# A third gate bank, mirrors one step late, and output products brought forward at the change to pairs

## The chip, the cores and the metric

The kernel runs on one core of a Trainium2 chip. The metric is the device time of one execution in microseconds (us). Medians of several executions are given, and all executions here are in the fast state (granted TensorE clock 0.997 to 1.000 of full speed). A profile is one execution. Its times are counted from the start of its span, and the span is about 2 us shorter than the time that is reported for the same execution.

## The reference, cut to what matters

```
X   = fft(fft(x, axis=1), axis=2).real      # x: 8 x 3008 x 256
gate = relu(X @ w_gate);  val = X @ w_val   # 256 -> 1536
out  = (gate * val) @ w_out                 # 1536 -> 256
```

The kernel works on 24 blocks (8 sequences, 3 blocks each) of up to 512 columns, and on 12 slices of 128 hidden units per block. A spectrum of real data is symmetric, so each block serves direct rows and mirrored rows. A gate is the sum of an even and an odd part; adding one further matmul with the odd weights times minus two (`wm`) into the same PSUM bank turns the direct gate into the mirrored one.

## The kernel before: the parts concerned

The names used below: t counts slices over all blocks, and the first block is t = 0 to 11. G(t) are the two gate matmuls, M(t) the gate's mirror matmul, W(t) the value's mirror matmul, V(t,0) and V(t,1) the two value matmuls. gs(t) and gm(t) are ScalarE's relus of the direct and the mirrored gate. direct_h and mirror_h are VectorE's products, and E(t) is VectorE's even part of the value, from t = 12 on. Output products are the matmuls of h with the output weights `wo`. Stage 1 and stage 2, transposes and weight folding prepare transforms and weights, and their matmuls stand between the others. The prelude is all that comes before the first gate matmul. A bank is the part of PSUM, the memory into which TensorE writes its sums, that holds one tile of 128 x 512 numbers.

```
psg = tile_pool(bufs=2)          # gate banks
pso = tile_pool(bufs=1)          # output banks, two tags
ps1 = singles.tile_pool(bufs=4)  # value banks of the first block, also of the prelude
# ... cut

def gate(t):
    G = Gt[t] = psg.tile([128, 512], F32, tag="g")
    matmul(G, wc[0], ..., start=True);  matmul(G, ws[0], ..., stop=True)
    scalar.activation(gs[t], G, Relu)
def mirror_gate(t):
    matmul(G of t, wm[0], ..., start=False)
    scalar.activation(gm[t], G of t, Relu)
# ... cut

for t in range(NF):                       # first block, one slice at a time
    if t:
        mirror_gate(t - 1)
    gate(t)
    value(t, 0)
    value(t, 1)
    direct_h(t, 1)
    if t:
        last_value(t - 1)                 # W(t-1), then mirror_h(t-1) on VectorE
    between(t)                            # weight folding, transposes, stage 2

for p in range(NF // 2, n + NF // 2):     # then pairs of slices
    t = 2 * p
    live = p < n
    if p <= n:
        mirror_gate(t - 1)
    if p == NF // 2:                      # the change to pairs, t = 12
        gate(t)
        last_value(t - 1)
        singles.close()                   # the value banks are given up ...
        psv = tile_pool(bufs=2)           # ... for two pair tiles of two banks each
    if live:
        value(t, 0)
        value(t + 1, 0)
        if p > NF // 2:
            gate(t)
    out_piece(t - NF, 0)                  # four output products of an earlier block
    between(t)
    # ... cut
```

## Time and profile before

| | before |
|---|---|
| time, median (range) of the 6 executions that the result was compared with | 625.03 us (624.44 to 625.51) |
| span of the profile | 623.1 us |
| TensorE busy | 612.1 us, 98% |
| first gate matmul starts | 21.56 us |
| M(12) starts | 52.19 us |

TensorE is busy nearly all the time, so time is gained only by closing gaps between matmuls. The records of matmuls overlap, so a gap shows in the starts of consecutive matmuls rather than in the busy share.

### The profile page before, as it was taken

Reading aid. Unit: us, or ns where it says so; the run is one execution under the profiler, and the core shown is the slowest. Engines: PE = TensorE matmul, PEld = TensorE weight load, DVE = VectorE, ACT = ScalarE, POOL = GpSimd, SP = SyncE. Lnnn points to the kernel's source line nnn. Section 1 sums busy time; section 2 is a strip of 40 time slices with the busy share of each in tenths; the row PEclk is TensorE's granted clock in tenths of the full one; section 3 lists DMA queues with packets and bytes.
Section 4 is the critical chain, followed back from the end, with each engine's and each line's share of the span. In section 5 each row is a group of like instructions: output and inputs, shape, how many; then the busy total and the mean of one; then the engine's idle time right before and its main releaser. Section 6 shows DMA issues by size and latency. Waiting matters only on the chain.

```text
span 623.1 us, 11916 instructions
## 1 busy us (share of the span) xinstructions
PE 612.1 (98%) x4252; PEld 409.3 (66%) x4284; DVE 536.5 (86%) x652; ACT 444.4 (71%) x855; POOL 520.2 (83%) x447
## 2 busy tenths in 40 slices
PE   8999999999999999999999999999999999999996
PEld 5345666666666666666667666766666666666665
DVE  7677898899889898988988998898988889899991
ACT  7677777777777767767777777767677676766660
POOL 8998998998898898899988998888988965555664
PEclk9999999999999999999999999999999999999998
DMA  8984282425452182613843255531822134112114
GB/s 169 241 163 114 83 220 77 123 66 169 118 145 71 41 228 79 155 36 89 221 102 90 66 162 126 138 77 34 223 82 59 34 86 124 52 34 67 34 35 99
DMA packets 42037, 67.44 MB, mean 108 GB/s; under 512 B 5877, under 2 KB 31774, under 8 KB 39962
## 3 DMA queue, kind: packets, MB, share of 16 engines
q1 hardware_dynamic: 37162, 50.61, 31.2%
q0 software_dynamic: 4656, 15.88, 10.8%
q8 instruction: 33, 0.54, 0.4%
q14 instruction: 26, 0.21, 0.1%
q10 hardware_dynamic: 160, 0.20, 0.1%
HBM read 38.85 MB, written 30.17 MB: 111 GB/s over the span
## 4 chain that ended last, share of the span: by engine, by line
PE 96%; DMA 1%; issue 1%; ACT 1%; DVE 1%; POOL 0%; POOLq 0%
PE po L685 40%; PE V L635 19%; PE G L619 10%; PE G L626 10%; PE G L620 10%; PE psw L335 2%; PE ps L164 2%; PE ps L273 2%; DMA hi<-in_x_dram,ixf 1%; PE ps L218 1%; PE pst L242 0%; PE ps L168 0%; ACT gs L621 0%; ACT gm L628 0%; DVE h L656 0%
## 5 line engine op out<-in xcount | busy, mean ns | idle before, releaser
L656 POOL TENSOR_TENSOR h<-gm,E 128x992 bf16<-128x992 f32 (+1 forms) x138 | 320.0, 2319 | 82.8 <-DVE E L663 52.0
L685 PE MATMUL po<-wo,h 128*128 128x256 bf16 (+2 forms) x2304 | 328.4, 272 | 0.4
L685 PEld LDWEIGHTS <-h 128*128 128x128 bf16 (+2 forms) x2304 | 231.4, 103 | 105.9
L628 ACT ACTIVATE gm<-G 128x496 f32<-128x496 f32 (+1 forms) x288 | 170.6, 592 | 94.2 <-PE G L626 87.2
L649 DVE TENSOR_TENSOR h<-gs,V 128x1024 bf16<-128x1024 f32 (+3 forms) x150 | 173.9, 1159 | 66.0 <-PE V L635 41.2
L642 DVE SCALAR_TENSOR_TENSOR E<-nb,af,V 128x496 f32<-128x496 bf16 (+1 forms) x276 | 190.2, 730 | 0.7 <-PE V L635 0.7
L621 ACT ACTIVATE gs<-G 128x497 f32<-128x497 f32 (+2 forms) x288 | 169.6, 589 | 23.7 <-PE G L620 23.7
L663 DVE SCALAR_TENSOR_TENSOR E<-E,V 128x992 f32<-128x992 f32 (+1 forms) x138 | 164.4, 1191 | 0.0
L619 PE MATMUL G<-pq,wc 128*128 128x496 bf16 (+2 forms) x286 | 107.2, 375 | 1.1
L626 PE MATMUL G<-pq,wm 128*128 128x496 bf16 (+1 forms) x288 | 107.9, 375 | 0.3
L620 PE MATMUL G<-pq,ws 128*128 128x497 bf16 (+2 forms) x288 | 107.9, 375 | 0.1
L635 PE MATMUL V<-pq,ws 128*128 128x496 bf16 (+2 forms) x280 | 83.7, 374 | 0.0
L635 PE MATMUL V<-pq,wc 128*128 128x496 bf16 (+2 forms) x267 | 80.9, 374 | 0.8 <-DVE h L656 0.8
L620 PEld LDWEIGHTS <-ws 128*128 128x128 bf16 x288 | 28.2, 98 | 32.6
L698 ACT COPY os<-po 128x512 f32<-128x512 f32 x63 | 36.9, 586 | 14.3 <-PE po L685 12.5
L115 POOL TENSOR_TENSOR eo<-xla 94x256 bf16<-94x256 f32 x56 | 40.7, 733 | 0.6
L635 PEld LDWEIGHTS <-wc 128*128 128x128 bf16 x288 | 28.2, 98 | 19.7 <-issue 1.3
L619 PEld LDWEIGHTS <-wc 128*128 128x128 bf16 x288 | 28.2, 98 | 19.1 <-issue 1.1
L179 ACT CAST t<-ps 96x512 bf16<-96x512 f32 x56 | 32.7, 584 | 4.0 <-PE ps L164 1.9
L115 POOL TENSOR_TENSOR eo<-xlb 94x256 bf16<-94x256 f32 (+1 forms) x42 | 34.5, 823 | 0.7
L112 POOL TENSOR_TENSOR xla<-xla,xha 94x510 f32<-94x510 f32 x28 | 32.9, 1175 | 2.2
L626 PEld LDWEIGHTS <-wm 128*128 128x128 bf16 x288 | 28.1, 98 | 4.4 <-issue 1.6
(140 smaller groups left out, 366.7 us busy)
## 6 DMA issues: line engine op xcount, KB each, us to landing
out_dram<-os SPq DMA_DIRECT2D x124, 128.0 KB
Td<-t SPq DMA_DIRECT2D x7, 768.0 KB
t<-Td SPq DMA_DIRECT2D x7, 768.0 KB
out_dram<-os SPq DMA_DIRECT2D x82, 64.0 KB
xla<-in_x_dram SPq DMA_DIRECT2D x7, 720.0 KB
xlb<-in_x_dram SPq DMA_DIRECT2D x6, 640.0 KB
nb<-Nd SPq DMA_DIRECT2D x23, 128.0 KB
out_dram<-os SPq DMA_DIRECT2D x40, 48.0 KB
```

The costliest lines, as they stand in the source:

```text
L115: yield eng.tensor_tensor(e1[:, :, k:k + H], x1[:, :, 0:H], free(x1, D, [DX, n], [-1, H]), op=op)
L619: nc.tensor.matmul(G[:, ds], lhsT=wc[0][:, fs], rhs=pq[:, 0, ds], start=True, stop=False)
L620: nc.tensor.matmul(G[:, ds], lhsT=ws[0][:, fs], rhs=pq[:, 1, ds], start=False, stop=True)
L621: nc.scalar.activation(pair(t, "gs")[:, t % 2, ds], G[:, ds], ACTF.Relu)
L626: nc.tensor.matmul(G[:, cols], lhsT=wm[0][:, f * 128:(f + 1) * 128], rhs=pqt[b, blk][:, 1, cols], start=False, stop=True, skip_group_check ...
L628: nc.scalar.activation(pair(t, "gm")[:, t % 2, cols], G[:, cols], ACTF.Relu)
L635: nc.tensor.matmul(o, lhsT=w[:, f * 128:(f + 1) * 128], rhs=pqt[b, blk][:, min(k, 1), cs], start=(k == 0), stop=(k > 0 or split(t)), skip_ ...
L642: nc.vector.scalar_tensor_tensor(pair(t, "E")[:, t % 2, cols], nbt[b, blk][:, cols], af[:, f:f + 1], pair(t, "V")[:, t % 2, cols], op0=ALU ...
L649: nc.vector.tensor_tensor(pair(t, "h")[:, k, 0, 0:ds.stop - ds.start], pair(t, "gs")[:, k, ds], val, op=ALU.mult)
L656: eng.tensor_tensor(free(pair(t, "h")[:], 1024 * (t % 2) + 512 + w - 1, [1024, n], [-1, w]), pair(t, "gm")[:, k, cols], val[:, :, cols], o ...
L663: nc.vector.scalar_tensor_tensor(E[:, :, cols], E[:, :, cols], 2.0, V[:, :, cols], op0=ALU.mult, op1=ALU.subtract)
L685: nc.tensor.matmul(po[0:m, i, :], lhsT=pair(t - f + ff, "h")[:, ff % 2, sg, g * 128:g * 128 + m], rhs=wo[:, ff, :], start=(ff == 0), stop= ...
```

## The change

Its intent is to take ScalarE's relu off TensorE's path in the first block: the mirror matmul of slice t-1 comes after the gates and values of slice t. The direct relu then has a whole step, and a gate bank lives longer. A third gate bank therefore comes out of the value pool; every third slice's gate goes into it, so that a bank is written again after three slices and not two. At the change to pairs, output products stand ahead of the value pair, which must wait for the value banks of the first block.

```diff
-    ps1 = singles.enter_context(tc.tile_pool(name="psf", bufs=4, space=PS))
+    ps1 = singles.enter_context(tc.tile_pool(name="psf", bufs=3, space=PS))
 # ... cut (def gate)
-        G = Gt[t] = psg.tile([128, 512], F32, tag="g", name="G")
+        third = t < NF and t % 3 == 2
+        G = Gt[t] = (ps1 if third else psg).tile([128, 512], F32, tag="g", name="G", bufs=1 if third else 2)
 # ... cut (first block)
     for t in range(NF):
-        if t:
-            mirror_gate(t - 1)
         gate(t)
         value(t, 0)
         value(t, 1)
         direct_h(t, 1)
         if t:
+            mirror_gate(t - 1)
             last_value(t - 1)
 # ... cut (pairs)
+        start = p == NF // 2
+        if start:
+            gate(t)
         if p <= n:
             mirror_gate(t - 1)
-        if p == NF // 2:
-            gate(t)
+        if start:
             last_value(t - 1)
-            singles.close()
-            psv = ctx.enter_context(tc.tile_pool(name="psv", bufs=2, space=PS))
-        if live:
+        elif live:
             value(t, 0)
             value(t + 1, 0)
-            if p > NF // 2:
-                gate(t)
+            gate(t)
 # ... cut: out_piece(t - NF, 0), between(t), direct_h; even() now only if not start
         out_piece(t - NF, 1)
+        if start:
+            singles.close()
+            psv = ctx.enter_context(tc.tile_pool(name="psv", bufs=2, space=PS))
+            for fn in (lambda k: value(k, 0), even):
+                fn(t)
+                fn(t + 1)
```

More of the change, by code (lines that the diff above doesn't have):

```diff
@@ L826 @@
             direct_h(t - 2, 2)
-        if live:
+        if live and not start:
             even(t)
```

## The prediction

> **What bounds the kernel now.** I read the page first (busy shares, the chain that ended last), then TensorE's list of waits, then the timeline of the stretch that the change touches, engine by engine, and the DMA view. Throughout, t counts the slices of the hidden dimension: steps 0 to 11 are the first block, "pairs" start at t = 12. M(t) is the mirror matmul of the gate (L626), W(t) the mirror matmul of the value (L635 with wm), gs and gm ScalarE's two relus (L621, L628), direct_h and mirror_h VectorE's two products (L649, L656).
>
> ```profile
> PE 612.1 (98%) x4252; PEld 409.3 (66%) x4284; DVE 536.5 (86%) x652; ACT 444.4 (71%) x855; POOL 520.2 (83%) x447
> PE 96%; DMA 1%; issue 1%; ACT 1%; DVE 1%; POOL 0%; POOLq 0%
> ```
>
> TensorE is 98% busy and 96% of the chain. Its waits by name come to 3 us in all, and only one of them lies where the change acts:
>
> ```profile
> PE V L635 <- DVE h L656: 0.8, 1, 0.8
> ```
>
> But a matmul's record is longer (0.37 us) than its spacing, so "busy" hides short stalls. The starts show them. TensorE from step 10 to the change to pairs:
>
> ```profile
> 46.36 0.37 PE L635 MATMUL V<-pq,wc 128*128 128x496 bf16 x1
> 46.56 0.37 PE L635 MATMUL V<-pq,ws 128*128 128x496 bf16 x1
> 46.77 0.37 PE L635 MATMUL V<-pq,wm 128*128 128x496 bf16 x1
> 47.25 0.37 PE L626 MATMUL G<-pq,wm 128*128 128x496 bf16 x1
> ...
> 48.76 0.37 PE L626 MATMUL G<-pq,wm 128*128 128x496 bf16 x1
> 49.19 0.38 PE L620 MATMUL G<-pq,ws 128*128 128x512 bf16 x1
> 49.47 0.37 PE L635 MATMUL V<-pq,wm 128*128 128x496 bf16 x1
> 50.67 0.59 PE L635 MATMUL V<-pq,wc 128*128 128x512 bf16 x2 [0.83 <-DVE h L656]
> 51.10 0.60 PE L685 MATMUL po<-wo,h 128*128 128x256 bf16 x4
> ```
>
> Spacing is 0.208 us for 496 columns and 0.215 for 512 (two of them from 50.67 to 51.10), but W to M is 0.48 (46.77 to 47.25): a hidden 0.27 us stall. (The first gate matmul at 48.97 has no record here.) ScalarE says why:
>
> ```profile
> 46.14 0.58 ACT L628 ACTIVATE gm<-G 128x496 f32<-128x496 f32 x1 [0.46 <-PE G L626]
> 46.62 0.58 ACT L621 ACTIVATE gs<-G 128x496 f32<-128x496 f32 x1
> 47.65 0.58 ACT L628 ACTIVATE gm<-G 128x496 f32<-128x496 f32 x1 [0.46 <-PE G L626]
> ```
>
> M(t-1) to gm(t-1) is 0.40 (47.25 to 47.65), gm(t-1) to gs(t) 0.48, gs(t) to M(t) 0.63 (46.62 to 47.25; gs must have read the gate bank before M adds to it). That loop is 1.51 to 1.52 us, exactly the step (45.73, 47.25, 48.76), while six matmuls need 6 x 0.208 = 1.25. VectorE, which ends the last wait:
>
> ```profile
> 48.74 0.67 DVE L649 TENSOR_TENSOR h<-gs,V 128x496 bf16<-128x496 f32 x1 [0.26 <-ACT gs L621]
> 49.33 1.28 DVE L656 TENSOR_TENSOR h<-gm,V 128x496 bf16<-128x496 f32 x2
> ```
>
> Its products follow each other every 0.59 us and release TensorE 0.73 after their start (49.47 - 48.74; the second L656 starts at 49.94 in the chain, and 49.94 + 0.73 = 50.67).
>
> **What the Trainium skill says.** "TensorE: Matmul & The Clock Gate", Wait — 56ns, not 53.3ns?: warm spacing is N / 2.4 GHz plus about 2.5 ns, so 209 and 216 ns; the trace has 208 and 215. "Perfetto Trace Analysis", Identifying the Most-Contended Engine, has matmul busy time as a bad metric because matmuls are pipelined; here 98% busy covers a step with 0.27 of 1.52 us idle. "PSUM — Partial Sum Buffer", PSUM bank collisions: semaphores must guard PSUM by bank and quadrant, so M cannot overlap the relu; the trace has M 0.05 us after gs ends (46.62 + 0.58 = 47.20). The same page, Specifications, gives eight banks: before 2 gate + 2 output + 4 value, after 3 + 2 + 3, so the third gate bank can only come from the values.
>
> **The change, part by part.** No work is added or removed: same matmuls, relus and products, in another order.
>
> (1) Steps 9 to 11. New order on TensorE: G(t) twice, V(t) twice, M(t-1), W(t-1). From a step's start: gs(t) at 0.208 + 0.41 = 0.62; M(t-1) at 0.83 needs gs(t-1), read one step ago (-0.63 + 0.63 = 0.0): no wait. gm(t-1) at 1.24. direct_h(t) at 0.62 + 0.61 = 1.23; mirror_h(t-1) at 1.24 + 0.61 = 1.85, done 2.44, before direct_h(t+1) at 2.48. W(t-1) at 1.04 needs direct_h(t-1): -0.02 + 0.73 = 0.71. Each fits, so the step becomes TensorE's 1.25. Removed: 0.26 before M(9), 0.27 before M(10), 0.26 before M(11), and about 0.05 before M(8), 0.84 in all.
>
> (2) Steps 0 to 8 carry 1.01 us weight-folding groups or transposes on TensorE besides. Apart from M(8), no M there waits measurably. Their gaps of about 0.1 us stand before the folding matmuls (24.70 + 0.208 = 24.91, next at 25.00) and at t = 6 VectorE's 0.2 on an output bank. These stay: 0.
>
> (3) Three value banks. V(t) reuses the bank of V(t-3), free after mirror_h(t-3): from the start of step t-3, 1.85 + 1.25 + 0.73 = 3.83, against V(t) at 3 x 1.25 + 0.42 = 4.17: 0.34 us to spare where the step is shortest, more elsewhere. In the prelude the rotation shortens too: the tightest reuse is the fourth transform tile, whose matmuls start after 13.05, on the first one's bank, copied out from 10.68 on, three copies in 1.28: about 2 us to spare. Cost: 0.
>
> (4) The change to pairs. Count from the end of step 11's issue (before: 48.50) to M(12). Before: 52.19 - 48.50 = 3.69, of which 2.36 is matmul time (M(11), W(11) 0.42; two gates, two values, one stage-1 pair 1.08; eight output matmuls of 0.109, 0.87); stalls 1.33 (0.26 counted in (1), 0.06 at W(11), 0.99 at V(12), rounding 0.02). After: G(12) 0 to 0.43; M(11) 0.43; W(11) at 0.64, but direct_h(11) starts at -0.02 and releases at 0.71, a wait of 0.08; then eight output matmuls and the stage-1 pair from 0.93 to 2.01. V(12) needs mirror_h(11). Here ScalarE takes gs(12) first, at 0.63, so gm(11) is at 0.63 + 0.48 = 1.11 and not at 0.84; mirror_h(11) at 1.11 + 0.61 = 1.72; released at 2.45. So TensorE still waits 2.45 - 2.01 = 0.44. V(12), V(13), then M(12) at 2.88. Saved: 3.69 - 2.88 = 0.81, of which 0.26 was counted.
>
> (5) A new small wait. The two E products (L642) start 0.63 after V(12) (51.30 - 50.67), at 3.08, 0.67 apart, and release their halves after about 0.79: 3.87 and 4.54. Before V(12,1) now lie only M(12), two gates, four output and two stage-1 matmuls (1.30), so V(12,1) issues at 4.18 without waiting and V(13,1) at 4.54 instead of 4.40: 0.15 lost.
>
> Sum: 0.84 + (0.81 - 0.26) - 0.15 = 1.24, say 1.2 us.
>
> (6) Does it reach the end? After 52 us TensorE issues without gaps: in the third block
>
> ```profile
> 76.40 1.04 PE L685 MATMUL po<-wo,h 128*128 128x256 bf16 x8
> ...
> 80.24 1.04 PE L685 MATMUL po<-wo,h 128*128 128x256 bf16 x8
> ...
> 84.09 1.04 PE L685 MATMUL po<-wo,h 128*128 128x256 bf16 x8
> ```
>
> a pair takes 3.84 us, and its work is 10 x 0.2085 + 16 x 0.109 = 3.83. So an earlier start moves everything after it, unless a transfer with its own clock holds it. Two could: the output weights (wo), issued at 36.59 and landing 10.3 us later, at 46.9, against a first output matmul moved from 51.10 to about 44.20 + 3 x 1.25 + 0.93 = 48.9; and GpSimd's folds for the next sequence, the first long done (40.7) and the fourth done at 50.5, needed around 56. GpSimd itself idles 1.51 us before its first product of pairs (58.11), so it can start that earlier by 1.2.
>
> **Rivals.** (a) VectorE binds: 2 x 0.59 = 1.17 of a 1.25 step leaves 0.08; with only three value banks a small lag becomes waits of V on L656. For it: the slack of 0.34. Against: it has idle in each step before. It would leave steps of about 1.4, half of (1): about 624.5. (b) The wait at the change moves rather than shrinks: gm(11) now queues behind gs(12). If both E products must be read before V(12,1), or the pool's release comes later, another 0.3 to 0.5 is lost: 624.5. (c) Output products cover the whole wait because the new pair's banks hang on earlier steps only: 0.44 better, 623.6. In the trace of before it waits for the last mirror_h, which speaks against it. (d) wo late: 2.0 us to spare; each us beyond it costs one: 624.5 to 625.5. (e) The gain is taken back later by a wait on GpSimd or a load: 625.3. Against: no such wait of TensorE over 0.2 us appears after 51 us.
>
> **Range and chances.** 625.28 - 1.2 = 624.1. The runs of before span 1.07 us, so the median alone is uncertain by some 0.4; rivals (a), (b), (d) reach up to 0.5 above, (c) 0.5 below. I take 623.2 to 625.0. Two per cent is 12.5 us, ten times the largest gain or loss that I can construct.
>
> **What would show it.** Right: in steps 9 to 11 six matmuls every 1.25 us, M without a gap, gs about 0.6 apart from gm; the first output matmul at about 48.9, before the value pair; a wait of V on L656 of about 0.3 named by the profile (0.4 by starts); M(12) at about 50.8; the end about 1.2 earlier; the period of 3.84 unchanged. Wrong: steps above 1.3 us, waits of V in the first block, a wait of the first output matmul on wo, or the distance from M(12) to the end (before: 623.1 - 52.19 = 570.9) grown.

## The result, and the profile after

| | before | after |
|---|---|---|
| time, median (range), 6 executions each | 625.03 us (624.44 to 625.51) | 623.91 us (623.17 to 624.23) |
| ratio, 95% interval | | 0.9982 (0.9969 to 0.9994) |
| span of the profile | 623.1 us | 622.2 us |
| first gate matmul starts | 21.56 us | 21.87 us |
| first gate to M(12) | 30.63 us | 29.30 us |
| M(12) to V(12,1) | 1.31 us | 1.66 us |
| first gate to the last unbroken run of output products | 585.22 us | 584.24 us |

A ratio compares the mean times of the runs, so it is not quite the ratio of the medians. The gain is 1.12 us by the medians. Within the profiles it is 0.98 us from the first gate matmul on (585.22 - 584.24).

The page of the changed kernel, busy share of TensorE and the chain that ended last:

```profile
PE 613.3 (99%) x4284; PEld 409.1 (66%) x4284; DVE 537.0 (86%) x652; ACT 444.9 (72%) x855; POOL 519.9 (84%) x447
PE 96%; DMA 1%; POOL 1%; DVE 1%; issue 0%; ACT 0%; POOLq 0%
```

The shares say next to nothing about a change of this size, and the busy times of TensorE (612.1 before, 613.3 here) can't be compared: before's profile lacks 32 matmul records (x4252 against x4284). TensorE's waits (engine, line, what it waited for: us in total, times, longest) say a little more:

```profile
PE V L636 <- DVE h L657: 0.3, 1, 0.3
...
PE V L636 <- DVE E L643: 0.2, 1, 0.2
```

The wait at the change to pairs has shrunk from 0.8 to 0.3, and one that was not there before, on E, has come. Two waits of the prelude on ScalarE (0.4 and 0.3) are new in this profile too; e0, the same kernel once more, has neither. (Lines moved by one: L636 was L635, L657 was L656, L643 was L642.) TensorE's timeline, one step and the change to pairs (start, duration, line, operation):

```profile
47.03 0.37 PE L620 MATMUL G<-pq,wc 128*128 128x496 bf16 x1
...
47.86 0.37 PE L627 MATMUL G<-pq,wm 128*128 128x496 bf16 x1
48.07 0.37 PE L636 MATMUL V<-pq,wm 128*128 128x496 bf16 x1
48.28 0.38 PE L620 MATMUL G<-pq,wc 128*128 128x512 bf16 x1
...
48.71 0.37 PE L627 MATMUL G<-pq,wm 128*128 128x496 bf16 x1
48.98 0.37 PE L636 MATMUL V<-pq,wm 128*128 128x496 bf16 x1
49.19 0.60 PE L686 MATMUL po<-wo,h 128*128 128x256 bf16 x4
...
50.74 0.59 PE L636 MATMUL V<-pq,wc 128*128 128x512 bf16 x2 [0.29 <-DVE h L657]
51.17 0.38 PE L627 MATMUL G<-pq,wm 128*128 128x512 bf16 x1
...
52.83 0.59 PE L636 MATMUL V<-pq,ws 128*128 128x512 bf16 x2 [0.20 <-DVE E L643]
```

The step is now 1.25 us (47.03 to 48.28) instead of 1.52, and the six matmuls in it stand 0.21 apart without a gap. The first output products start at 49.19, ahead of the value pair. The pair still waits until 50.74, though the eight output products and the stage-1 pair before it were issued by about 50.29 (the second four start at 49.85, and four take 4 x 0.109). ScalarE and VectorE over the same stretch say what it waits for:

```profile
48.27 0.58 ACT L629 ACTIVATE gm<-G 128x496 f32<-128x496 f32 x1
48.91 0.60 ACT L622 ACTIVATE gs<-G 128x512 f32<-128x512 f32 x1
49.41 0.58 ACT L629 ACTIVATE gm<-G 128x496 f32<-128x496 f32 x1
```

```profile
48.89 0.67 DVE L657 TENSOR_TENSOR h<-gm,V 128x496 bf16<-128x496 f32 x1
50.02 0.67 DVE L657 TENSOR_TENSOR h<-gm,V 128x496 bf16<-128x496 f32 x1 [0.46 <-PE ps L164]
51.37 1.41 DVE L643 SCALAR_TENSOR_TENSOR E<-nb,af,V 128x512 f32<-128x512 bf16 x2 [0.68 <-PE V L636]
```

gs(12) goes first at 48.91, gm(11) follows at 49.41, the last mirror_h at 50.02 (0.61 after gm(11)), and the value pair at 50.74, 0.72 after that. The profile names a stage-1 matmul as what VectorE waited for at 50.02; gm(11), exactly one relu latency earlier, fits better, and e5 below tests it.

Afterwards nothing is lost or won. The output products that stood at 76.40, 80.24 and 84.09 before now stand at 75.73, 79.57 and 83.42:

```profile
75.73 1.04 PE L686 MATMUL po<-wo,h 128*128 128x256 bf16 x8
...
83.42 1.04 PE L686 MATMUL po<-wo,h 128*128 128x256 bf16 x8
```

Each is 0.67 earlier, which is 0.98 less the 0.31 by which this execution's first gate matmul came later.

### The profile page after: what moved, and what is told of

The parts are those of the page before. It is cut to its first block, busy times and chain, and to the rows that moved or that the text cites. A ratio compares the mean times of both kernels' runs of the same rounds, so it can differ in the third digit from the quotient of the medians.

```text
span 622.2 us, 11959 instructions
## 1 busy us (share of the span) xinstructions
PE 613.3 (99%) x4284; PEld 409.1 (66%) x4284; DVE 537.0 (86%) x652; ACT 444.9 (72%) x855; POOL 519.9 (84%) x447
## 4 chain that ended last, share of the span: by engine, by line
PE 96%; DMA 1%; POOL 1%; DVE 1%; issue 0%; ACT 0%; POOLq 0%
PE po L686 40%; PE V L636 20%; PE G L620 10%; PE G L621 10%; PE G L627 10%; PE psw L335 2%; PE ps L164 2%; PE ps L273 2%; DMA lo<-in_x_dram 1%; POOL hi L133 0%; PE pst L242 0%; PE ps L218 0%; PE ps L168 0%; DVE E L643 0%; POOL lo L130 0%
## 5 line engine op out<-in xcount | busy, mean ns | idle before, releaser
L657 POOL TENSOR_TENSOR h<-gm,E 128x992 bf16<-128x992 f32 (+1 forms) x138 | 319.9, 2318 | 82.0 <-DVE E L664 52.9
L643 DVE SCALAR_TENSOR_TENSOR E<-nb,af,V 128x496 f32<-128x496 bf16 (+1 forms) x276 | 190.1, 730 | 1.1 <-PE V L636 0.7
L620 PE MATMUL G<-pq,wc 128*128 128x497 bf16 (+2 forms) x288 | 108.0, 375 | 0.0
L636 PE MATMUL V<-pq,wc 128*128 128x497 bf16 (+2 forms) x288 | 85.5, 375 | 0.3 <-DVE h L657 0.3
L636 PE MATMUL V<-pq,ws 128*128 128x497 bf16 (+2 forms) x288 | 85.4, 375 | 0.2 <-DVE E L643 0.2
L699 ACT COPY os<-po 128x512 f32<-128x512 f32 x63 | 36.9, 586 | 14.3 <-PE po L686 12.0
L636 PEld LDWEIGHTS <-wc 128*128 128x128 bf16 x288 | 28.2, 98 | 19.0 <-issue 0.5
```

What stands on the lines that cost most here:

```text
L620: nc.tensor.matmul(G[:, ds], lhsT=wc[0][:, fs], rhs=pq[:, 0, ds], start=True, stop=False)
L636: nc.tensor.matmul(o, lhsT=w[:, f * 128:(f + 1) * 128], rhs=pqt[b, blk][:, min(k, 1), cs], start=(k == 0), stop=(k > 0 or split(t)), skip_ ...
L643: nc.vector.scalar_tensor_tensor(pair(t, "E")[:, t % 2, cols], nbt[b, blk][:, cols], af[:, f:f + 1], pair(t, "V")[:, t % 2, cols], op0=ALU ...
L657: eng.tensor_tensor(free(pair(t, "h")[:], 1024 * (t % 2) + 512 + w - 1, [1024, n], [-1, w]), pair(t, "gm")[:, k, cols], val[:, :, cols], o ...
```

## The experiments

Theory: the 1.52 us step of the first block was the loop M, gm, gs, M through ScalarE's queue, and the new order opens it, for which the third gate bank is needed. What remains at the change is gm(11) standing behind gs(12). The new wait of V(12,1) is on both E products. The rivals were that the bank alone or the order alone does it, that one of the two parts gives everything, that the change delays the prelude, and that the remaining wait is for something other than gm(11).

All eight kernels gave correct results. Each call's four kernels ran on one chip, five times each, with nine executions of before (median 625.12 us in the first call, 624.82 in the second). The intervals of the ratios are about 0.13% (0.8 us) wide to each side, so the times alone rarely decide. The distances within a profile decide: in the one kernel that was profiled twice (after and e0) they repeat to 0.01. Each of the other kernels has one profile. "Span to the end" below is the distance from the first gate matmul to the start of the last unbroken run of 84 output products; all distances are differences of starts in the timeline and in the chain that ended last.

| kernel | time, median us | ratio to before | first gate to M(12) | M(12) to V(12,1) | span to the end | against before |
|---|---|---|---|---|---|---|
| before | 625.12 / 624.82 | | 30.63 | 1.31 | 585.22 | |
| after (first profile) | 623.91 | 0.9982 | 29.30 | 1.66 | 584.24 | -0.98 |
| e0_after_again | 623.99 | 0.9987 | 29.31 | 1.66 | 584.25 | -0.97 |
| e1_block_only | 623.80 | 0.9983 | 29.85 | 1.30 | 584.43 | -0.79 |
| e2_change_only | 624.83 | 1.0000 | 29.82 | 1.66 | 584.76 | -0.46 |
| e3_banks_only | 625.00 | 1.0006 | 30.63 | 1.31 | 585.22 | 0.00 |
| e4_two_gate_banks | 625.82 | 1.0015 | 31.17 | 1.66 | 586.11 | +0.89 |
| e5_mirror_first | 623.29 | 0.9978 | 28.85 | 1.66 | 583.79 | -1.43 |
| e6_even_late | 624.77 | 0.9995 | 29.30 | 1.31 | 584.89 | -0.33 |
| e7_both_waits | 622.83 | 0.9968 | 28.85 | 1.75 | 583.44 | -1.78 |

### e1_block_only: the first block alone

After, with the `for p` loop of before put back unchanged:

```diff
-        if start:
-            gate(t)
         if p <= n:
             mirror_gate(t - 1)
-        if start:
+        if p == NF // 2:
+            gate(t)
             last_value(t - 1)
-        elif live:
+            singles.close()
+            psv = ctx.enter_context(tc.tile_pool(name="psv", bufs=2, space=PS))
+        if live:
             value(t, 0)
             value(t + 1, 0)
 # ... cut: the rest of the loop as before
```

> Only the first block is changed (three gate banks, three value banks, mirrors one step late); the change to pairs keeps the order of before. Theory (the relu loop set the step, and M(11) at the change was its last turn): steps 9 to 11 every 1.25 us as in after; from the end of step 11 to M(12) 3.43 us instead of 3.69 (M(11) no longer waits 0.26; V(12) still waits for the last mirror_h, now about 1.0 after W(11)); first gate matmul to M(12) 30.63 - 0.53 - 0.26 = 29.84. V(12,1) does not wait, so the last output matmul comes about 0.8 earlier against the first gate than in before: 0.8 us faster. Rival (the gain of after lies only in the output products brought forward): within 0.2 us of before.

Measured: 623.80 us, ratio 0.9983 (0.9970 to 0.9997). First gate to M(12) is 29.85 (expected 29.84), and the span to the end is 0.79 shorter. The rival, that the output products give the whole gain, falls. The block alone brings 0.79 of after's 0.98. By the medians it would be 1.32 (625.12 - 623.80), within the scatter of the times.

### e2_change_only: the change to pairs alone

Before, with the `for p` loop of after; the first block and the banks stay:

```diff
 # against after
-    ps1 = singles.enter_context(tc.tile_pool(name="psf", bufs=3, space=PS))
+    ps1 = singles.enter_context(tc.tile_pool(name="psf", bufs=4, space=PS))
-        third = t < NF and t % 3 == 2
-        G = Gt[t] = (ps1 if third else psg).tile(...)
+        G = Gt[t] = psg.tile([128, 512], F32, tag="g", name="G")
     for t in range(NF):
+        if t:
+            mirror_gate(t - 1)
         gate(t)
 # ... cut
         if t:
-            mirror_gate(t - 1)
             last_value(t - 1)
```

> Only the change to pairs is reordered; the first block keeps two gate banks, four value banks and the order of before. Theory: steps 9 to 11 stay at 1.51; from the end of step 11 to M(12) 2.88 instead of 3.69; V(12,1) then waits about 0.35 as in after (1.66 from M(12) instead of 1.31). Net 0.81 - 0.35 = 0.46 us faster than before; first gate to M(12) 29.8. This and the block alone together give 1.25, more than the 0.98 of after against the first gate, since the 0.26 before M(11) is counted in both. Rival (parts add up): 0.98 - 0.8 = 0.2 faster. Rival (it needs the late mirror to work at all): no change.

Measured: 624.83 us, ratio 1.0000 (0.9987 to 1.0014), which the times cannot tell from no change. The profile can: M(12) is at 29.82 from the first gate, V(12,1) 1.66 after M(12), and the span to the end is 0.46 shorter, each as expected. The two parts alone come to 0.79 + 0.46 = 1.25. Together they give 0.98, because both remove the 0.26 that M(11) waited.

### e3_banks_only: the banks alone

After's pools and `gate`, before's two loops:

```diff
     for t in range(NF):
+        if t:
+            mirror_gate(t - 1)
         gate(t)
 # ... cut
         if t:
-            mirror_gate(t - 1)
             last_value(t - 1)
 # ... cut: and the loop of pairs as before
```

> Only the banks are changed (three gate, three value), every order is that of before. Theory (the order sets the relu loop, the third bank only makes the new order possible): steps 9 to 11 stay at 1.51 to 1.52, M(12) 30.63 from the first gate, time within 0.2 us of before. Rival (the gate bank was what the matmuls waited for): steps of 1.25, 0.8 us faster. Rival (three value banks cost something): a wait of V on the mirror product, slower by 0.3 or more.

Measured: 625.00 us, ratio 1.0006 (0.9992 to 1.0019). TensorE's timeline has the old step, W at 46.67 and M only 0.48 later (the next M is at 48.66, 1.51 after that):

```profile
46.67 0.37 PE L636 MATMUL V<-pq,wm 128*128 128x496 bf16 x1
47.15 0.37 PE L627 MATMUL G<-pq,wm 128*128 128x496 bf16 x1
```

A third gate bank without the new order is worth nothing, and three value banks instead of four cost nothing (585.22 both).

### e4_two_gate_banks: the orders alone

After, with two gate banks and four value banks:

```diff
-    ps1 = singles.enter_context(tc.tile_pool(name="psf", bufs=3, space=PS))
+    ps1 = singles.enter_context(tc.tile_pool(name="psf", bufs=4, space=PS))
-        third = t < NF and t % 3 == 2
-        G = Gt[t] = (ps1 if third else psg).tile(...)
+        G = Gt[t] = psg.tile([128, 512], F32, tag="g", name="G")
```

> All orders of after, but two gate banks and four value banks. Theory: G(t+1) now reuses the bank of G(t-1), whose gm is taken 1.24 into step t and read by 1.24 + 0.63 = 1.87; so steps 9 to 11 take 1.87 instead of 1.26, a wait of the first gate matmul on gm of about 0.6 in each of three; steps 0 to 7, with their 1 us of weight folding, hide it. First gate to M(12) 29.30 + 3 x 0.61 = 31.1; time 1.8 slower than after, some 0.9 slower than before. Rival (order alone gives the gain): as after, 0.98 faster than before.

Measured: 625.82 us, ratio 1.0015 (1.0002 to 1.0029), 0.89 longer than before in the profile. The wait has moved from M to G:

```profile
47.68 0.37 PE L619 MATMUL G<-pq,wc 128*128 128x496 bf16 x1 [0.46 <-ACT gm L628]
...
49.56 0.38 PE L619 MATMUL G<-pq,wc 128*128 128x512 bf16 x1 [0.46 <-ACT gm L628]
```

The step is 1.88 us (expected 1.87). So the order needs the bank, and the bank needs the order; either one alone gains nothing.

### e0_after_again: the changed kernel once more

No edit.

> The changed kernel once more, unedited. Expected: first gate matmul to M(12) 29.30 and to the last output matmul as in its first profile within 0.05 us; the start of the first gate matmul itself (21.56 in before, 21.87 in after) differs from execution to execution by some 0.3, because a transfer of the input ends the wait ahead of it, not because of the value banks. If the later start belongs to the change, it is again about 0.3 later than before. Time 0.9 to 1.2 faster than before.

Measured: 623.99 us, ratio 0.9987 (0.9973 to 1.0000), which is 0.83 faster than before by the medians and so a little less than expected. The distances repeat to 0.01. The first gate matmul starts at 21.76 here, 0.20 later than in before's profile, which by itself would not decide. Over all ten profiles it starts between 21.23 and 22.09, and both ends of that range are kernels with three value banks (e5 and e1); with four they are 21.56, 21.64 and 21.27. In the profile of after the chain that ended last shows what decided:

```profile
6.51 6.32 DMA lo<-in_x_dram
...
12.85 0.61 ACT back L199
13.46 0.41 ACT t L232
```

A part of the input lands at 12.83 (6.51 + 6.32), ScalarE reverses it, and only then evacuates the transform tile whose bank the next matmul wants at 13.91. In before's profile the same ScalarE copy started at 12.41 and the same matmul at 13.64. By the program's alternation that bank is an output bank, of which both kernels have two. So the later start in the first profile of after is a transfer's landing, and no delay by the value banks shows. In e0's own profile the chain runs through another transfer, of the gate's weights, which lands at 14.92: which transfer decides changes from execution to execution.

### e5_mirror_first: M(11) ahead of G(12)

```diff
-        if start:
-            gate(t)
         if p <= n:
             mirror_gate(t - 1)
         if start:
+            gate(t)
             last_value(t - 1)
```

> After, with M(11) ahead of the two gate matmuls of t = 12. Theory (the rest of the wait at the change is gm(11) queued behind gs(12)): gm(11) about 0.47 after the end of step 11 instead of 1.11, the last mirror_h at 1.19, released 1.92, before the output products end at 2.01: V(12) does not wait, M(12) at about 2.45 instead of 2.89 from the end of step 11; V(12,1) waits as in after (0.35). About 0.45 us faster than after, 1.4 than before. Rival (the wait is for the bank release or for W(11)): M(12) at 2.89 still, time as after.

Measured: 623.29 us, ratio 0.9978 (0.9964 to 0.9992). ScalarE takes gm(10) and gm(11) one after the other, gs(12) after them:

```profile
47.64 1.06 ACT L629 ACTIVATE gm<-G 128x496 f32<-128x496 f32 x2
48.58 0.60 ACT L622 ACTIVATE gs<-G 128x512 f32<-128x512 f32 x1
```

On TensorE the second four output products start at 49.21 and the value pair at 49.65, 0.44 later, which is their own time: no wait. M(12) comes at 28.85 from the first gate, 0.45 earlier than in after, and the span to the end is 0.45 shorter. So the remaining wait was gm(11) behind gs(12); the rivals (the bank release, W(11)) fall.

### e6_even_late: the second E product after V(12,1)

```diff
-            for fn in (lambda k: value(k, 0), even):
-                fn(t)
-                fn(t + 1)
+            value(t, 0)
+            value(t + 1, 0)
+            even(t)
 # ... cut
             value(t, 1)
+            if start:
+                even(t + 1)
             value(t + 1, 1)
```

> After, with the second E product (of t = 13) placed after V(12,1) in the program. In after V(12,1) waited 0.35 and started 0.79 after the second E product, not the first. Theory A (the wait is on both only because both stood ahead of it in the program): V(12,1) without a wait, 1.31 from M(12); V(13,1) then waits about 0.13 for the second E product; 0.2 us faster than after. Theory B (halves of the pair's value tile cannot be told apart): the second E product is held until V(12,1) has ended, starts about 0.4 after it, and V(13,1) comes about 1.2 after V(12,1): 0.5 to 0.7 slower than after.

Measured: 624.77 us, ratio 0.9995 (0.9982 to 1.0009), 0.65 slower than after in the profile (584.89 against 584.24). Theory B is right. TensorE and VectorE:

```profile
52.69 0.38 PE L636 MATMUL V<-pq,ws 128*128 128x512 bf16 x1
53.91 0.38 PE L636 MATMUL V<-pq,ws 128*128 128x512 bf16 x1 [0.84 <-DVE E L643]
```

```profile
51.58 0.75 DVE L643 SCALAR_TENSOR_TENSOR E<-nb,af,V 128x512 f32<-128x512 bf16 x1 [0.68 <-PE V L636]
53.10 0.75 DVE L643 SCALAR_TENSOR_TENSOR E<-nb,af,V 128x512 f32<-128x512 bf16 x1 [0.78 <-PE V L636]
```

V(12,1) now goes without a wait, 1.31 after M(12). But the second E product, which reads the other half of the pair's tile, waits for it and starts 0.41 after it, and V(13,1) is 1.22 later than V(12,1). The two halves of a pair's value tile are ordered as one. That is an ordering in the program as built, seen by its effect; that the chip itself would demand it is not shown.

### e7_both_waits: both remaining waits removed

```diff
-        if start:
-            gate(t)
         if p <= n:
             mirror_gate(t - 1)
         if start:
+            gate(t)
             last_value(t - 1)
 # ... cut
+        if start:
+            out_piece(t + 1 - NF, 1)
         if live:
             value(t, 1)
             value(t + 1, 1)
-        out_piece(t + 1 - NF, 1)
+        if not start:
+            out_piece(t + 1 - NF, 1)
```

> After, with M(11) ahead of the gate matmuls of t = 12, and with the second four output products of t = 1 ahead of V(12,1). Theory: both remaining waits go, 0.44 and 0.35: the distance from the first gate to the first output product after V(13,1) is shorter than in after by about 0.8; time 1.8 us faster than before, 0.8 faster than after. Rival (the second wait is passed on to the next pair, since V(12,1) and with it VectorE's product of the pair comes no earlier): 0.45 faster than after, a new wait of some 0.3 in the following pair.

Measured: 622.83 us, ratio 0.9968 (0.9954 to 0.9981); after had 623.99. This version beats both kernels, by 1.78 us against before and 0.80 against after in the profile. V(12,1) follows the four output products without a wait, and the value pair V(14,0), V(15,0) follows at 52.65 without one either:

```profile
51.57 0.60 PE L686 MATMUL po<-wo,h 128*128 128x256 bf16 x4
52.01 0.59 PE L636 MATMUL V<-pq,ws 128*128 128x512 bf16 x2
...
52.65 0.59 PE L636 MATMUL V<-pq,wc 128*128 128x512 bf16 x2
```

V(14,1) comes at 55.92, 0.22 after the stage-1 pair ahead of it (55.70), which is that pair's own time. The rival, that the wait is passed on to the next pair, falls.

## Why the prediction was right

The time was predicted as 624.1, range 623.2 to 625.0, and is 623.91. That the two agree within 0.2 us is in part luck. The prediction took 1.2 from 625.28, the median of the three executions of before that were known then; with three more it is 625.03, so the base alone moved by 0.25. The range ends only 0.03 below that median. The time alone therefore tests little, and the steps are tested in the profiles:

1. **Steps 9 to 11, 0.84 predicted.** The 0.26, 0.27 and 0.26 came as foreseen: from the start of step 9 to the end of step 11's issue is 3.77 (44.51 to 48.28) against 4.56 from M(8) to M(11) before (44.20 to 48.76), a gain of 0.79. The 0.05 before M(8) did not come. The distance from the twelve small matmuls ahead of it is 0.38 in both kernels (43.82 to 44.20, 44.13 to 44.51), so that gap was not M waiting for a relu.
2. **Steps 0 to 8 unchanged, 0.** Right: the folding matmuls keep the gap of about 0.1 ahead of them (25.00 + 0.21 to 25.31 in after), and the 0.2 on VectorE at t = 6 is still there.
3. **Three value banks, 0.** Right; the banks alone leave every distance as it was (e3).
4. **The change to pairs, 0.81.** From the end of step 11's issue to M(12) is 2.89 (48.28 to 51.17) against 2.88 predicted. Counted from there, gm(11) was at 1.13 (predicted 1.11), the last mirror_h at 1.74 (1.72), V(12) at 2.46 (2.45). e5 shows that this was the cause, and not only a number that fits.
5. **The new small wait, 0.15 predicted, 0.35 measured.** This is the step that failed, in kind and in size. The prediction had each of the two E products release its own half of the pair's value tile, so V(12,1) would not wait and V(13,1) would wait 0.15. V(12,1) waited for the second E product: it started 1.46 after the first E product (51.37 to 52.83), which is 0.67 to the second E product and 0.79 for its release. Rival (b) had named this condition, and e6 shows it. One sign that the prediction had given for being wrong came true with it: from M(12) to the last unbroken run of output products is 554.94 (606.11 - 51.17) against 554.59 before (606.78 - 52.19), longer by the same 0.35.
6. **It reaches the end.** Right: the products of the third block stand 0.67 earlier, and so does the start of the last unbroken run (606.78 before, 606.11 after). The output weights landed at 36.9 + 10.3 = 47.2 and were first used at 49.19, so rival (d) had 2.0 us to spare. Rival (a) did not come about: no value matmul waits in the block. Nor did (c), since V(12) still waited, or (e).

The sum as it should have been is 0.79 + (0.80 - 0.26) - 0.35 = 0.98, where the 0.80 is 3.69 - 2.89 and the 0.26 before M(11) is counted once. The predicted sum of 1.24 was 0.26 too large: 0.20 in step 5, 0.05 before M(8) and 0.01 in step 4. The medians' 1.12, and 0.83 (624.82 - 623.99), lie on both sides of it; the six executions of before differ by 1.07 us, and those of after by 1.06. The start of the first gate matmul alone varies by 0.86 over the ten profiles.

## What to carry to other kernels

When the busiest engine shows 98%, read the starts of its instructions: a step that takes exactly the latency of a loop through another engine's queue (here 0.40 + 0.48 + 0.63 = 1.51) is a stall that busy shares hide. Such a loop is opened by order and buffers together: here the bank alone gained nothing and the order alone lost 0.89 us. When filler work is pulled in front of a wait, look at what the filler no longer stands in front of: here four output products were all that was missing before the second value product, and moving them was worth 0.35 us.

## What the Trainium skill lacked or had wrong

- "Perfetto Trace Analysis", Optimization Strategy, says that consistent bubbles on the engine that should be saturated can mean that there is not enough SBUF or PSUM for the next tile. Here the repeating bubble of 0.27 us was of another kind: one more PSUM bank alone left it as it was (e3: 585.22 in both). The page could add that a bubble may be a loop through another engine's queue, to be tested by adding the buffer alone.
- No page was found that gives the time from a read of PSUM to the release of the matmul that waits for it. The runs show 0.63 us from the start of a relu of 496 columns (0.05 after its record ends), 0.73 from the start of VectorE's product (0.06 after it ends), and 0.40 from the start of a matmul to the relu that reads it. With these numbers the three handovers at the change to pairs were worked out to 0.02 us.
- "PSUM — Partial Sum Buffer", PSUM bank collisions, asks for semaphores by bank and quadrant. It does not say that a tile of two banks may be ordered as a whole by the program that is built: here the halves lie in two banks, and still the second E product started only 0.41 us after the start of a matmul into the other half, for which it had waited (e6).
